# Two of four W2 operands of an expert product start 32 bytes further on, with a table of scan constants moved to another pool

## The chip, the cores and the metric

The kernel runs on one core of a Trainium2 chip. The metric is the time that the device takes for one execution, in microseconds (us), as the median of several runs. The two kernels compute the same thing with the same instructions; only places in the on-chip memory (SBUF, 128 partitions, addresses counted in bytes within a partition) differ.

## What is computed

An attention with a decaying state gives x (3072 tokens of 384 numbers). A first mixture multiplies `(x @ w1) * (x @ w2)` by `w3` and `w_out`. A second one weighs 8 experts by a gate that is balanced eight times over rows and columns, and this is where most of the time goes:

```python
def _moe2_ref(x, w_gate, w1, w2):
    logits = x @ w_gate
    P = np.exp(logits - logits.max())
    for _ in range(8):
        P /= P.sum(1, keepdims=True) + 1e-09
        P /= P.sum(0, keepdims=True) + 1e-09
        P *= N / E
    out = np.zeros((N, D), dtype=np.float32)
    for e in range(E):                       # 8 experts
        h = np.maximum(x @ w1[e], 0.0)       # 384 -> 1024
        out += P[:, e:e + 1] * (h @ w2[e])   # 1024 -> 384
    return out
```

## The kernel before

**Stages.** For about 400 us the attention runs beside the first mixture (`START` and the loop over `s`). Then `N` = 64 phases follow, 8 experts times 2 halves of the inner 1024 times 4 batches of 768 tokens. A phase has two products on TensorE. The *first product* (`phase`, `z_prod`, tiles `zp`) is `x @ w1` in 15 combined block products; its operands are `w1c` (stationary) and `xc` (streamed, 256 columns). After it, ScalarE and VectorE make from each block of `h` a high part `hh` and a low part `hl` (`h_hi`, `h_lo`). The *second product* (`y_fill`, tiles `yp`) is `h @ w2`. It belongs to the phase before and is mixed in between the steps of the first product by a written-out table (`YN`), in `unit`s.

**One unit.** `unit(b_, h_, i, j)` issues three matmuls into the same accumulator: `hh` against the high part of W2 (`w2h`), `hh` against its low part (`w2l`), and `hl` against `w2h`. The 128x128 slice of `hh` or `hl` is stationary; the W2 row block `w_[:, i, :]`, 384 columns of 4 bytes = 1536 bytes a partition, is streamed. `j` runs over 0 and 1 and picks one of a pair of W2 tiles, so the streamed tiles follow each other as h0, l0, h0, h1, l1, h1 and so on (0 and 1 are the pair's first and second tile). A phase has 24 units, 72 matmuls; 64 phases have 4608.

**W2 tiles.** `sp_w2(i)` makes `w2h{k}` and `w2l{k}`, k = i mod 4, each of 2 x 384 numbers (3072 bytes a partition). k = 0 and 1 are one pair and live in the pool `m1`, which is stacked from the upper end of the SBUF; k = 2 and 3 are the other pair, in the pool `m2` at the lower end. Pairs alternate.

**Places.** A pool lays its tiles one behind the other. `spaced` asks for an unused tile ahead of a tag if the table `GAPS` names it, of so many 4-byte numbers a partition, or behind it for a tag with `+`. In the program as built, all streamed operands of both products (`w2h`, `w2l`, `xc`) begin 96 bytes past a multiple of 256, and all stationary ones (`hh`, `hl`, `w1c`) 160 bytes past one. In blocks of 64 bytes, each stream begins 32 bytes into a block and ends 32 bytes into one. In the first mixture the operands (`xhl`, `gh`, `gl` and `w1h`, `w1l`, `w2h`, `w2l`, `w34h`, `w34l`) all begin 96 bytes past a multiple of 256.

**The scans' constants.** `d1` (529 numbers of 2 bytes) is an operand of the two scans of the attention (`scan_f`, `scan_g`). It lies in `const`, the lowest pool, which stays for the whole kernel.

Of the kernel before, what the change touches and what calls it, by code (L numbers as in the profile page):

```python
# [11 lines left out]
F32 = mybir.dt.float32  # L12
F32R = mybir.dt.float32r
BF16 = mybir.dt.bfloat16
# [47 lines left out]
def tile_rwkv_moe_sinkhorn_moe(  # L62
# [18 lines left out]
    nc = tc.nc  # L81
    B, H, S, D = SHAPE
    NT, DM = out.shape
    P = 128
# [21 lines left out]
    def mm(o, lhsT, rhs, start, stop, pos=None, tr=False, skip=False):  # L106
# [5 lines left out]
        if tr:  # L112
# [3 lines left out]
    const = ctx.enter_context(tc.tile_pool(name="const", bufs=1))  # L116
    ident = const.tile([P, P], F32, name="ident")
    mask = const.tile([P, DP], F32, name="mask")
    eye = const.tile([P, DP], F32, name="eye")
    d1 = const.tile([P, 16 * 33 + 1], BF16, name="d1")  # L120
    GP = 32
    gate = const.tile([P, KD, GP], F32, name="gate")
    lowb = const.tile([P, 1], F32, name="lowb")
# [5 lines left out]
    nc.gpsimd.memset(ident, 1.0)  # L129
    nc.gpsimd.affine_select(out=ident, in_=ident, compare_op=ALU.is_equal, fill=0.0,  # L130
                            base=0, pattern=[[-1, P]], channel_multiplier=1)
    nc.vector.memset(d1, 0.0)
    nc.vector.memset(d1[:, 0:528].rearrange("p (b s) -> p b s", s=33)[:, :, 0:1], 1.0)
    nc.vector.memset(d1[:, 528:529], 1.0)
    nc.gpsimd.memset(mask, 1.0)
    for c in range(2):
        nc.scalar.activation(eye[64 * c:64 * c + 64, :], ident[64 * c:64 * c + 64, 64 * c:64 * c + 64], AF.Copy)
# [7 lines left out]
    mw = st_mw.enter_context(tc.tile_pool(name="mw", bufs=1))  # L145
    st_attn = ExitStack()
    att = st_attn.enter_context(tc.tile_pool(name="att", bufs=1))
    st_ps = ExitStack()
    ps = st_ps.enter_context(tc.tile_pool(name="ps", bufs=1, space=PSUM))
    st_pa = ExitStack()  # L150
# [467 lines left out]
        return sums, high, low  # L618

    w1raw, w2raw, w1c, w2c, xc, xd = {}, {}, {}, {}, {}, {}  # L620
    GAPS = {'hh': 32, 'hl+': 32, 'w2h2': 16, 'w2l3+': 16, 'w1c00': 16, 'xc0': 48, 'w1c10': 16, 'xc1': 48, 'w1c01': 16, 'w1c13+': 16}

    def spaced(pool, shape, dtype, tag, name, **kw):
        n_ = GAPS.pop(tag, 0)
        if n_:
            pool.tile([P, n_], F32, name="gap_" + tag)
        t = pool.tile(shape, dtype, tag=tag, name=name, **kw)
        n_ = GAPS.pop(tag + "+", 0)
        if n_:
            pool.tile([P, n_], F32, name="gap_after_" + tag)  # L630
        return t
# [619 lines left out]
```

## Time and profile before

| what | value |
|---|---|
| median of 3 runs | 1918.84 us (1918.38 to 1919.31) |
| the profiled execution | 1919.88 us |
| its span, first to last instruction | 1918.2 us |
| TensorE busy in the span | 1891.9 us, 99% |
| VectorE, ScalarE, GpSimd busy | 72%, 36%, 34% |
| granted TensorE clock | 1.00, the 2.4 GHz level |

TensorE has two rows in a profile: PE, the streaming matmul, and PEld, the load of the stationary operand, which runs beside it. The recorded length of a matmul includes its way through the array and overlaps with the next one, so what one costs is the distance from its start to the next start. The median is 1.04 us below the profiled execution, and the span 1.68 us below it.

### The profile page before, as it was taken

Reading aid. Unit: us, or ns where it says so; the run is one execution under the profiler, and the core shown is the slowest. Engines: PE = TensorE matmul, PEld = TensorE weight load, DVE = VectorE, ACT = ScalarE, POOL = GpSimd, SP = SyncE. Lnnn points to the kernel's source line nnn. Section 1 sums busy time; section 2 is a strip of 40 time slices with the busy share of each in tenths; the row PEclk is TensorE's granted clock in tenths of the full one; section 3 lists DMA queues with packets and bytes.
Section 4 is the critical chain, followed back from the end, with each engine's and each line's share of the span. In section 5 each row is a group of like instructions: output and inputs, shape, how many; then the busy total and the mean of one; then the engine's idle time right before and its main releaser. Section 6 shows DMA issues by size and latency. Waiting matters only on the chain.

```text
span 1918.2 us, 38115 instructions
## 1 busy us (share of the span) xinstructions
PE 1891.9 (99%) x15499; PEld 1843.2 (96%) x15499; DVE 1377.1 (72%) x2409; ACT 685.0 (36%) x1322; POOL 648.2 (34%) x867
## 2 busy tenths in 40 slices
PE   6999999999999999999999999999999999999999
PEld 3799999999999999999999999999999999999999
DVE  7865777766887887766767777767676777767666
ACT  6733333344333333333333333333333333333322
POOL 6766666634431323132222222222323231312200
PEclk9999999999999999999999999999999999999999
DMA  9622444346655555555655555545555555555563
GB/s 369 238 85 92 136 133 139 110 146 223 233 183 200 183 201 192 197 185 179 217 176 205 180 203 183 205 173 197 187 192 192 193 190 196 196 181 185 176 204 120
DMA packets 90494, 353.76 MB, mean 184 GB/s; under 512 B 10384, under 2 KB 34256, under 8 KB 64592
## 3 DMA queue, kind: packets, MB, share of 16 engines
q1 hardware_dynamic: 90320, 351.34, 52.8%
q8 instruction: 122, 2.00, 0.4%
q14 instruction: 52, 0.43, 0.1%
HBM read 329.67 MB, written 20.45 MB: 183 GB/s over the span
## 4 chain that ended last, share of the span: by engine, by line
PE 94%; DVE 2%; DMA 2%; ACT 1%; issue 0%; SPq 0%; DVEq 0%; ACTq 0%
PE yp L114 41%; PE zp L114 34%; PE po L114 5%; PE pa L114 5%; PE pb L114 5%; PE yt L114 1%; DMA raw<-in_moe_w_dram 1%; PE w34ps L114 1%; PE sc L114 1%; PE trn L114 1%; DMA nat_kn<-in_kn_dram 1%; PE up L114 0%; PE pl L114 0%; DVE cvp L229 0%; DVE Sn L384 0%
## 5 line engine op out<-in xcount | busy, mean ns | idle before, releaser
L114 PE MATMUL zp<-xc,w1c 128*128 128x256 f32 x5760 | 793.0, 277 | 0.9 <-DVE ct L906 0.6
L114 PEld LDWEIGHTS zp<-xc,w1c 128*128 128x128 f32 x5760 | 766.5, 188 | 4.4 <-DVE ct L909 1.0
L114 PE MATMUL yp<-w2h,hl 128*128 128x384 f32 x1536 | 515.3, 336 | 0.6 <-DVE hl L903 0.6
L114 PE MATMUL yp<-w2l,hh 128*128 128x384 f32 x1536 | 514.6, 335 | 0.0
L114 PE MATMUL yp<-w2h,hh 128*128 128x384 f32 x1536 | 513.1, 334 | 0.0
L898 ACT ACTIVATE hh<-ct 128x512 fp32r<-128x512 f32 x384 | 236.1, 630 | 526.5 <-DVE ct L906 265.9
L906 DVE TENSOR_TENSOR ct<-ct,zp 128x512 f32<-128x512 f32 x576 | 377.0, 680 | 47.2 <-PE zp L114 42.4
L616 POOL TENSOR_TENSOR w1c<-w1s,w1c 128x512 fp32r<-128x512 f32 (+1 forms) x120 | 127.4, 1062 | 779.6 <-ACT w1c L612 779.6
L913 ACT ACTIVATE ct<-zp 128x512 f32<-128x512 f32 x256 | 153.4, 599 | 440.8 <-PE zp L114 440.8
L114 PEld LDWEIGHTS yp<-w2h,hl 128*128 128x128 f32 x1536 | 288.3, 188 | 1.1 <-DVE hl L903 0.9
L114 PEld LDWEIGHTS yp<-w2h,hh 128*128 128x128 f32 x1536 | 288.4, 188 | 0.2 <-issue 0.2
L114 PEld LDWEIGHTS yp<-w2l,hh 128*128 128x128 f32 x1536 | 288.3, 188 | 0.0
L1078 DVE SCALAR_TENSOR_TENSOR acc<-yp,Pm,acc 128x384 f32<-128x384 f32 x336 | 205.5, 612 | 103.6 <-PE yp L114 103.5
L903 DVE SCALAR_TENSOR_TENSOR hl<-ct,hh 128x512 fp32r<-128x512 f32 x384 | 275.8, 731 | 0.0
L909 DVE TENSOR_TENSOR ct<-ct,zp 128x512 f32<-128x512 f32 x128 | 87.9, 687 | 162.9 <-PE zp L114 162.9
L909 DVE TENSOR_TENSOR ct<-zp,ct 128x512 f32<-128x512 f32 x128 | 88.3, 690 | 74.4 <-ACT ct L913 60.8
L616 POOL TENSOR_TENSOR w1c<-w1raw,w1c 128x128 fp32r<-128x128 f32 (+1 forms) x90 | 56.5, 628 | 195.4 <-ACT w1c L612 195.4
L608 POOL TENSOR_TENSOR w1s<-w1raw 128x128 f32<-128x128 f32 x240 | 120.8, 524 | 0.2
L483 POOL TENSOR_TENSOR gl<-gs,gh 128x384 fp32r<-128x384 f32 x64 | 74.2, 1161 | 109.5 <-ACT gh L479 109.5
L114 PE MATMUL pa<-xhl,w1h 128*128 128x384 f32 x384 | 101.7, 345 | 0.9 <-ACT w34s L255 0.9
L114 PE MATMUL pb<-xhl,w2h 128*128 128x384 f32 x384 | 98.1, 336 | 0.4 <-DVE cv L230 0.4
L474 DVE TENSOR_TENSOR gs<-pb,asb 128x384 f32<-128x384 f32 x64 | 35.4, 553 | 72.0 <-PE pb L114 50.1
(130 smaller groups left out, 1905.3 us busy)
## 6 DMA issues: line engine op xcount, KB each, us to landing
xc<-xd SPq DMA_DIRECT2D x192, 1024.0 KB, 4.9
xc<-xd SPq DMA_DIRECT2D x64, 768.0 KB, 4.2
xd<-x2s SPq DMA_DIRECT2D x53, 256.0 KB, 2.8
w1raw<-in_e_w_dram SPq DMA_DIRECT2D x32, 384.0 KB, 3.2
w2raw<-in_e_w_dram SPq DMA_DIRECT2D x32, 384.0 KB, 3.1
raw<-in_moe_w_dram SPq DMA_DIRECT2D x8, 1024.0 KB, 10.1
nat_w<-in_w_dram SPq DMA_DIRECT2D x24, 264.5 KB, 3.5
nat_k<-in_kt_dram SPq DMA_DIRECT2D x24, 256.0 KB, 4.1
```

The lines of the kernel that those rows point to most:

```text
L114: nc.tensor.matmul(o, lhsT, rhs, start=start, stop=stop, **kw)
L474: nc.vector.tensor_tensor(t, m_t.pop(("pb", blk, f)), m_t.pop(("asb", blk, f)), op=ALU.mult)
L483: nc.gpsimd.tensor_tensor(gl[:, f, :], m_t.pop(("gs", blk, f)), gh[:, f, :].bitcast(F32), op=ALU.subtract)
L608: eng.tensor_tensor(tmp_[:, many.index(r), :], at_(a), at_(b), op=ALU.add if sg == 1 else ALU.subtract)
L616: eng.tensor_tensor(lo[:, d0:d1, :], sv, hi[:, d0:d1, :].bitcast(F32), op=ALU.subtract)
L898: nc.scalar.activation(hh, src, AF.Relu)
L903: nc.vector.scalar_tensor_tensor(hl, src, 0.0, hh.bitcast(F32), op0=ALU.max, op1=ALU.subtract)
L906: nc.vector.tensor_tensor(o, a, b_, op=ALU.add)
L909: nc.vector.tensor_tensor(o, a, b_, op=ALU.subtract)
L913: nc.scalar.activation(t, src, AF.Copy)
L1078: nc.vector.scalar_tensor_tensor(dst, yp, so["Pm"][:, tt, e:e + 1], dst, op0=ALU.mult, op1=ALU.add)
```

## The change

The table gets four more entries, each for one W2 tile: a gap of 8 numbers (32 bytes) ahead of the low part of a pair's first tile, and one of 56 (224 bytes) ahead of the low part of its second, so that 256 bytes are inserted for a pair. The room comes from `d1`, which leaves `const` for the attention's pool `att`; an unused tile of 64 bytes stays at its old place. The three memsets that fill `d1` are written further down.

```diff
-    d1 = const.tile([P, 16 * 33 + 1], BF16, name="d1")
+    const.tile([P, 16], F32, name="gap_const")
@@
-    nc.vector.memset(d1, 0.0)
-    nc.vector.memset(d1[:, 0:528].rearrange("p (b s) -> p b s", s=33)[:, :, 0:1], 1.0)
-    nc.vector.memset(d1[:, 528:529], 1.0)
@@
     att = st_attn.enter_context(tc.tile_pool(name="att", bufs=1))
+    d1 = att.tile([P, 16 * 33 + 1], BF16, name="d1")
+    nc.vector.memset(d1, 0.0)
+    nc.vector.memset(d1[:, 0:528].rearrange("p (b s) -> p b s", s=33)[:, :, 0:1], 1.0)
+    nc.vector.memset(d1[:, 528:529], 1.0)
@@
-    GAPS = {'hh': 32, 'hl+': 32, 'w2h2': 16, 'w2l3+': 16, 'w1c00': 16, ...
+    GAPS = {'hh': 32, 'hl+': 32, 'w2l0': 8, 'w2l1': 56, 'w2h2': 16, 'w2l2': 8, 'w2l3': 56, 'w2l3+': 16, 'w1c00': 16, ...
```

The places in the two programs as built, in bytes past a multiple of 256:

| tile | before | after |
|---|---|---|
| `w2h0`, `w2h2` (high part, first of a pair) | 96 | 96 |
| `w2l0`, `w2l2` (low part, first) | 96 | 128 |
| `w2h1`, `w2h3` (high part, second) | 96 | 128 |
| `w2l1`, `w2l3` (low part, second) | 96 | 96 |
| `xc`, `hh`, `hl`, `w1c` | 96, 160, 160, 160 | the same |
| buffers of the attention | | each 64 bytes further on |
| `d1` | 128 | 96 |

Other tiles move by whole multiples of 256 bytes (256, 768 or 1024 down) or not at all. On every engine the instructions stand in the same order and carry the same waits. On TensorE, at the first two units of the second product (the number behind a tile's name counts tiles in the program; the figure ahead of it, 0 or 1, is the tile of the pair), before:

```order
L114 MATMUL yp_6332<-w2h0_6153,hh_6283 128x384
L114 MATMUL yp_6332<-w2l0_6154,hh_6283 128x384
L114 MATMUL yp_6332<-w2h0_6153,hl_6284 128x384
L114 MATMUL yp_6332<-w2h1_6197,hh_6283 128x384
L114 MATMUL yp_6332<-w2l1_6198,hh_6283 128x384
L114 MATMUL yp_6332<-w2h1_6197,hl_6284 128x384
```

The same place after:

```order
L114 MATMUL yp_6335<-w2h0_6154,hh_6286 128x384
L114 MATMUL yp_6335<-w2l0_6156,hh_6286 128x384
L114 MATMUL yp_6335<-w2h0_6154,hl_6287 128x384
L114 MATMUL yp_6335<-w2h1_6199,hh_6286 128x384
L114 MATMUL yp_6335<-w2l1_6201,hh_6286 128x384
L114 MATMUL yp_6335<-w2h1_6199,hl_6287 128x384
```

Nothing moved; the numbers differ because gaps count as tiles. In these six rows the streamed operands begin 96, 96, 96, 96, 96, 96 bytes past a multiple of 256 before, and 96, 128, 96, 128, 96, 128 after: from matmul to matmul the start alternates between the middle of a 64-byte block and its beginning.

## Rows read from the trace of the kernel before

**Rows 1.** The page's first part: busy time, share of the span, instructions.

```profile
PE 1891.9 (99%) x15499; PEld 1843.2 (96%) x15499; DVE 1377.1 (72%) x2409; ACT 685.0 (36%) x1322; POOL 648.2 (34%) x867
```

**Rows 2.** The page's chain that ended last, by engine.

```profile
PE 94%; DVE 2%; DMA 2%; ACT 1%; issue 0%; SPq 0%; DVEq 0%; ACTq 0%
```

**Rows 3.** Busy time in the stretch of the 64 phases: length, engines, clock, DMA.

```profile
464.20:1914.80 1450.60, 1449.50 (x10331) 1444.95 (x10329) 1045.70 (x1715) 477.45 (x883) 365.95 (x589) 1.00 0.55 191
```

**Rows 4.** TensorE's waits from 464 us on: us in total, times, longest.

```profile
PE yp L114 <- DVE hl L903: 0.6, 1, 0.6
PE zp L114 <- DVE ct L909: 0.3, 1, 0.3
```

**Rows 5.** The page's groups of both products: busy, mean ns, idle before.

```profile
L114 PE MATMUL zp<-xc,w1c 128*128 128x256 f32 x5760 | 793.0, 277 | 0.9 <-DVE ct L906 0.6
...
L114 PE MATMUL yp<-w2h,hl 128*128 128x384 f32 x1536 | 515.3, 336 | 0.6 <-DVE hl L903 0.6
L114 PE MATMUL yp<-w2l,hh 128*128 128x384 f32 x1536 | 514.6, 335 | 0.0
L114 PE MATMUL yp<-w2h,hh 128*128 128x384 f32 x1536 | 513.1, 334 | 0.0
```

**Rows 6.** Timeline of TensorE in mid-stage: start us, length us, matmul, how many.

```profile
1001.20 0.85 PE L114 MATMUL zp<-xc,w1c 128*128 128x256 f32 x6
1001.88 0.33 PE L114 MATMUL yp<-w2h,hh 128*128 128x384 f32 x1
1002.05 0.34 PE L114 MATMUL yp<-w2l,hh 128*128 128x384 f32 x1
1002.23 0.34 PE L114 MATMUL yp<-w2h,hl 128*128 128x384 f32 x1
...
1003.27 0.34 PE L114 MATMUL yp<-w2h,hl 128*128 128x384 f32 x1
1003.44 0.28 PE L114 MATMUL zp<-xc,w1c 128*128 128x256 f32 x1
```

**Rows 7.** The same view, last 78 matmuls of the second product, first and last.

```profile
1901.00 0.33 PE L114 MATMUL yp<-w2h,hh 128*128 128x384 f32 x1
...
1914.35 0.34 PE L114 MATMUL yp<-w2h,hl 128*128 128x384 f32 x1
```

**Rows 8.** Matmuls of `yp` by operand: duration ns min/median/max, first and last start.

```profile
L114 PE MATMUL yp<-w2h,hh x1536: 332/332/443, 464.3 to 1914.0; 128*128 128x384 f32 x192
...
L114 PE MATMUL yp<-w2l,hh x1536: 332/335/339, 464.5 to 1914.2; 128*128 128x384 f32 x192
```

**Rows 9.** Timeline of TensorE in the first mixture's last product.

```profile
403.51 0.33 PE L114 MATMUL po<-gh,w34l 128*128 128x384 f32 x1
...
404.55 0.33 PE L114 MATMUL po<-gh,w34l 128*128 128x384 f32 x1
```

**Rows 10.** VectorE's timeline: one scan from each of `nat_w`'s two buffers.

```profile
120.65 1.25 DVE L279 TENSOR_TENSOR_SCAN Ft<-nat_w,d 128x528 f32<-128x528 f32 x1
```

**Rows 11.** The same view, a later stretch: the other buffer's turn.

```profile
129.25 1.26 DVE L279 TENSOR_TENSOR_SCAN Ft<-nat_w,d 128x528 f32<-128x528 f32 x1 [0.72 <-POOL Rt L312]
```

**Rows 12.** The memsets of `d1` and the scans that read it.

```profile
L283 DVE TENSOR_TENSOR_SCAN Gt<-nat_w,d x24: 1242/1582/2300, 3.6 to 377.6; 128x527 f32<-128x527 f32 x24
L279 DVE TENSOR_TENSOR_SCAN Ft<-nat_w,d x24: 1232/1490/2100, 4.8 to 375.3; 128x528 f32<-128x528 f32 x24
L132 DVE MEMSET d<- x1: 499/499/499, 1.1 to 1.1; 128x529 bf16 x1
```

More of the change, by code (lines that the diff above doesn't have):

```diff
@@ L620, in tile_rwkv_moe_sinkhorn_moe @@
     w1raw, w2raw, w1c, w2c, xc, xd = {}, {}, {}, {}, {}, {}
-    GAPS = {'hh': 32, 'hl+': 32, 'w2h2': 16, 'w2l3+': 16, 'w1c00': 16, 'xc0': 48, 'w1c10': 16, 'xc1': 48, 'w1c01': 16, 'w1c13+': 16}
+    GAPS = {'hh': 32, 'hl+': 32, 'w2l0': 8, 'w2l1': 56, 'w2h2': 16, 'w2l2': 8, 'w2l3': 56, 'w2l3+': 16, 'w1c00': 16, 'xc0': 48, 'w1c10': 16, 'xc1': 48, 'w1c01': 16, 'w1c13+': 16}
     def spaced(pool, shape, dtype, tag, name, **kw):
```

## The prediction, made before the result was known

> **What bounds the kernel now.** Read the busy shares first: TensorE is busy 99% of the span, VectorE 72%, the others far less [rows 1], and the chain of work that ended last lies on TensorE for 94% [rows 2]. That could still hide a stage with another limit, so look at the stage that the change touches. In the 1450.6 us of the 64 phases TensorE is busy for 1449.5 [rows 3], and its list of waits there has two entries, of 0.6 and 0.3 us [rows 4]. Nothing else sets the time of this stage: it is the number of matmuls times the distance from one start to the next. VectorE is idle for 1450.6 - 1045.7 = 404.9 us of it.
>
> The distances come from the timeline. Six matmuls of the first product take 1001.20 to 1001.88, 0.68 / 6 = 113.3 ns each; nine of the second take 1001.88 to 1003.44, 1.56 / 9 = 173.3 ns [rows 6]. The last 78 of the second product, with nothing between them, give 77 distances in 13.35 us, 173.4 ns [rows 7]. The clock granted is 1.00 [rows 3], its 2.4 GHz level, at which 256 columns are 106.7 ns and 384 are 160.0. So a matmul of the first product pays 6.7 ns (16 clocks) beyond its columns and one of the second 13.3 ns (32 clocks). The check: 5760 x 113.3 + 4608 x 173.3 = 652.6 + 798.6 = 1451.2 us with the counts of [rows 5], the length of the stage. 4608 x 13.3 = 61.3 us is all that a better place for W2 could win, if every overhead went.
>
> **What the change adds, removes and moves.** No instruction, no wait and no transfer is added, taken away or reordered on any engine, SP's and GpSimd's queues among them; so no wait can take the place of another except through a changed duration. Three things have a new place.
>
> *The memsets and scans of the constants.* The three memsets follow the same VectorE instruction as before, the big one 499 ns long [rows 12]. The 48 scans read `d1` from a start that is 32 bytes into a 64-byte block instead of at its beginning. Does VectorE care? The two buffers of `nat_w` lie one 32 bytes into a block and the other at the beginning of one, and a scan from each takes 1.26 us [rows 11] and 1.25 us [rows 10] when GpSimd leaves it alone: a difference of 10 ns on 48 scans, 0.5 us of VectorE's time, beside a TensorE that waits elsewhere. I take nothing; were the scans late, the bound is 0.5 us either way.
>
> *The buffers of the attention and the tiles that go down by 256, 768 or 1024 bytes.* These keep their place to the next multiple of 64 or of 256. I take nothing: the second product and the first mixture's last product have their stationary operand at 160 and 96 past a multiple of 256, the streamed one at 96 in both, and both run at the same pace, 6 distances in 1.04 us, 173.3 ns, in the latter [rows 9]. A shift by whole 64-byte blocks between the two operands has no price for a stream of 384 columns.
>
> *The W2 tiles.* This is the whole of the sum. `w2l` of a pair's first tile is streamed in 768 of the 1536 matmuls of hh on w2l, `w2h` of the second in 768 + 768 of the other two groups [rows 5]: 2304 matmuls, half of the product, begin at the start of a 64-byte block instead of 32 bytes into it. No row of the trace shows a streamed operand of this kind in such a place, so the price must be bounded. Below: it may lose all its overhead, 13.3 ns, or 2304 x 13.3 = 30.6 us. Above: nothing excludes a loss, and the nearest size for one is the step in which the overheads come. 6.7 and 13.3 ns are two and four steps of 3.3 ns, which is 8 clocks or 32 bytes of a stream; the recorded lengths of the second product's matmuls also come in two sizes that differ by 3 ns, 332 and 335 [rows 8]. A shift by just 32 bytes should act in such steps.
>
> Which way? Half-used blocks are the argument for a gain. 1024 bytes that begin 32 into a block touch 17 blocks of 64, and 17 x 16 clocks = 272 = 113.3 ns, the first product's distance to the clock. 1536 bytes touch 25 blocks, 166.7 ns, and the row shows 173.3: one block too many, as if the stream were taken in a piece of 256 columns and one of 128 (17 + 9 = 26 blocks). So the fit is good but not complete, and a fixed price of 16 clocks for each piece of up to 256 columns fits the same two numbers with no role for the start. I therefore take the smallest step for the forecast: one step of 3.3 ns on each of the 2304, 7.7 us. Against the profiled execution that is 1919.9 - 7.7 = 1912.2 us; its time stood 1.04 us above the median of the runs, so 1911.2 us for the median. TensorE's gain isn't taken back by another engine: VectorE's 404.9 us of idle time cover it many times.
>
> A page of the Trainium skill speaks against this. SBUF — State Buffer, section Specifications (TRN2), gives SBUF lines of 16 bytes and asks for at least two hits in a line. A start at 96 and one at 128 are both at the beginning of such a line, so by that rule the streams cost what they cost, and the time stays at 1918.8 us. No row here shows whether 16 bytes or 64 is the unit that a stream pays for.
>
> **The rivals.** *The start doesn't matter.* The overhead is a fixed price of each piece or of the handover between matmuls, and a stream costs 173.3 ns wherever it begins: 1918.8 us. For it: that 64 bytes make no difference between [rows 6] and [rows 9], and that the fixed price fits the two distances. Against it: only that the half block does so too.
>
> *All of the overhead goes.* If half blocks are the whole cause, an aligned stream costs 24 x 16 clocks = 160.0 ns, and 30.6 us go: 1888.2 us. For it, 17 x 16; against it, the block too many, and that some fixed price for a matmul would have to be nil.
>
> *Slower: the handover meets the same half block.* Before, a stream's last 32 bytes lie in the first half of a block and the next stream's first in the second half: the halves alternate through the handover. After, they meet in the same half at nearly every handover of the second product: h0 ends in a first half and l0 begins in one, l0 ends in a second half and h0 begins in one. If the two halves are read in turn and a repeat costs one step, it costs 3.3 ns at 2304 handovers if one kind of repeat is bad, +7.7 us or 1926.5 us, and at all 4608 if both are, +15.4 us or 1934.2 us. It decides as soon as more repeats cost a step than shifted streams save one. For it: the step is 32 bytes of stream. Against it: before, the halves alternate already and four steps are paid all the same.
>
> **How the numbers follow.** One or two steps off the shifted streams: 0.37 (two steps would be 1903.5 us); all of the overhead: 0.11; no effect: 0.25; one step more on half of the handovers: 0.18; on all: 0.09. The likeliest gives 1911.2 us. A range of 8 in 10 leaves out the largest gain (0.11) and the largest loss (0.09): from three steps saved, 1895.8, to 1926.5 with the spread of the runs, so 1895 to 1928 us. Both signs hold much of this; the forecast's own range is 1903 to 1912. What a measurement of this kernel can tell from no change is about 0.2%, 3.8 us. Faster by more than that: 0.37 + 0.11 = 0.48; within it 0.25; slower 0.18 + 0.09 = 0.27.
>
> **What would show it.** In the profile of the changed kernel the last 78 matmuls of the second product should take 77 distances of 173.4 - 1.7 = 171.7 ns on average, 13.22 us instead of 13.35; 160-ns distances on every other matmul would speak for the half blocks, 173.3 throughout for the fixed price, and more for the repeat. The first product must keep 113.3 ns, and the first 464 us must not move by more than 0.5 us. I am wrong in the mechanism if a matmul on an unshifted tile changes its distance, and in the bound if the gain stands in TensorE's distances but not in the time.

## The result: slower, and mostly where nothing was moved

The changed kernel takes 1939.03 us, median of four runs (1938.82 to 1939.78), beside 1918.78 us for the kernel before (1918.38 to 1919.31): a ratio of 1.0103, 95% interval 1.0091 to 1.0116. The profiled execution of after is the run of 1939.78 us; its span is 1938.1 us, 19.9 us more than before's 1918.2.

The page of after, first part (busy time, share of the span, instructions), beside [rows 1], and its groups of both products (busy us, mean ns of one, idle before), beside [rows 5]:

```profile
PE 1911.3 (99%) x15499; PEld 1864.0 (96%) x15499; DVE 1381.7 (71%) x2409; ACT 687.2 (35%) x1322; POOL 647.0 (33%) x867
...
L114 PE MATMUL zp<-xc,w1c 128*128 128x256 f32 x5760 | 807.2, 280 | 0.9 <-DVE ct L907 0.6
...
L114 PE MATMUL yp<-w2h,hh 128*128 128x384 f32 x1536 | 518.5, 338 | 0.0
L114 PE MATMUL yp<-w2h,hl 128*128 128x384 f32 x1536 | 517.2, 337 | 0.5 <-DVE hl L904 0.5
L114 PE MATMUL yp<-w2l,hh 128*128 128x384 f32 x1536 | 517.0, 337 | 0.0
```

TensorE is as full as before and busy for 19.4 us longer. The largest group to grow is `zp`, the first product: 793.0 to 807.2 us, though neither its streams nor its stationary tiles moved. The three groups of `yp` gain 9.7 us together (records of neighbouring matmuls overlap, so the groups add up to more than the 19.4). TensorE's waits in the 64 phases are still two (us in total, times, longest), as in [rows 4], so no wait has come in:

```profile
PE yp L114 <- DVE hl L904: 0.5, 1, 0.5
PE zp L114 <- DVE ct L910: 0.3, 1, 0.3
```

Now the timeline of TensorE in after (start us, length us, matmul, how many), where [rows 6] had 113.3 and 173.3 ns:

```profile
600.90 0.87 PE L114 MATMUL zp<-xc,w1c 128*128 128x256 f32 x6
601.61 0.34 PE L114 MATMUL yp<-w2h,hh 128*128 128x384 f32 x1
...
602.66 0.84 PE L114 MATMUL zp<-xc,w1c 128*128 128x256 f32 x6
603.34 0.33 PE L114 MATMUL yp<-w2h,hh 128*128 128x384 f32 x1
...
604.38 0.87 PE L114 MATMUL zp<-xc,w1c 128*128 128x256 f32 x6
605.08 0.34 PE L114 MATMUL yp<-w2h,hh 128*128 128x384 f32 x1
```

Six matmuls of the first product take 0.71, 0.68 and 0.70 us: 118, 113 and 117 ns each. Below, a *stretch* is a run of matmuls of one product with none of the other between them, and a *rhythm* the distance that such a run keeps. It is one kernel, one set of places, and two rhythms; a stretch that begins in one mostly stays in it. The last 78 matmuls of the second product, which answer [rows 7]:

```profile
1920.90 0.34 PE L114 MATMUL yp<-w2h,hh 128*128 128x384 f32 x1
...
1934.25 0.34 PE L114 MATMUL yp<-w2h,hl 128*128 128x384 f32 x1
```

That is 77 distances in 13.35 us, 173.4 ns (173.3 from the exact starts), as before, although half of these streams have moved. On average the second product, left alone, runs as it did. Single distances don't: they go from 171 to 176 ns, where before shows 173 and 174 behind the first one.

Where the 19.9 us lie, from the start times of all matmuls sorted by neighbours (all distances of each kind added up, after minus before): matmuls of `zp` +13.9 us; the first matmul of `yp` behind a stretch of `zp`, 170 ns before and some 175 after, +4.1; the other matmuls of `yp` +2.4. From these 20.4 goes half a microsecond by which the first `zp` starts earlier (441.3 instead of 441.8 us).

The kernel before, and e1 too, gave two values at the same granted clock, about 1919 and about 1929 us; the higher has no profile and no known cause, and while e5 to e8 were taken it was the only one (1928.74 us), so for those four the spans and distances count here and not the ratio (e8's would be 0.9978).

### The profile page after: what moved, and what is told of

It is laid out like the page before. It is cut to its first block, busy times and chain, and to the rows that moved or that the text cites. A ratio compares the mean times of both kernels' runs of the same rounds, so it can differ in the third digit from the quotient of the medians.

```text
span 1938.1 us, 38115 instructions
## 1 busy us (share of the span) xinstructions
PE 1911.3 (99%) x15499; PEld 1864.0 (96%) x15499; DVE 1381.7 (71%) x2409; ACT 687.2 (35%) x1322; POOL 647.0 (33%) x867
## 4 chain that ended last, share of the span: by engine, by line
PE 95%; DVE 2%; DMA 1%; ACT 1%; issue 0%; SPq 0%; DVEq 0%; ACTq 0%
PE yp L114 41%; PE zp L114 35%; PE po L114 5%; PE pa L114 5%; PE pb L114 5%; PE w34ps L114 1%; PE yt L114 1%; PE sc L114 1%; PE trn L114 1%; DMA nat_kn<-in_kn_dram 1%; PE up L114 1%; DMA raw<-in_moe_w_dram 0%; PE pl L114 0%; DVE Sn L385 0%; DVE cvp L230 0%
## 5 line engine op out<-in xcount | busy, mean ns | idle before, releaser
L114 PE MATMUL zp<-xc,w1c 128*128 128x256 f32 x5760 | 807.2, 280 | 0.9 <-DVE ct L907 0.6
L114 PEld LDWEIGHTS zp<-xc,w1c 128*128 128x128 f32 x5760 | 776.7, 188 | 3.5 <-DVE ct L910 0.9
L114 PE MATMUL yp<-w2h,hh 128*128 128x384 f32 x1536 | 518.5, 338 | 0.0
```

Source lines behind the costliest of these rows:

```text
L114: nc.tensor.matmul(o, lhsT, rhs, start=start, stop=stop, **kw)
```

## The experiments

A place is told in bytes past a multiple of 256, and the difference is the stationary tile's place minus the stream's. Which tile is loaded while a stream runs can be read from the trace: the load for a matmul starts together with the matmul ahead of it. In run e6 (below), the timeline of the weight loads, and of the matmuls:

```profile
601.43 0.83 PEld L114 LDWEIGHTS zp<-xc,w1c 128*128 128x128 f32 x6
602.20 0.19 PEld L114 LDWEIGHTS yp<-w2h,hh 128*128 128x128 f32 x1
```

```profile
601.43 0.34 PE L114 MATMUL yp<-w2h,hl 128*128 128x384 f32 x1
601.61 0.87 PE L114 MATMUL zp<-xc,w1c 128*128 128x256 f32 x6
602.31 0.34 PE L114 MATMUL yp<-w2h,hh 128*128 128x384 f32 x1
```

The load for the first `zp` begins at 601.43, with the last `yp`, and that for the first `yp` at 602.20, with the last `zp`. So there are four differences: within the first product (w1c and xc), from the first to the second (hh is loaded beside xc), within the second (hh or hl and W2), from the second to the first (w1c is loaded beside W2). Before, all four are 160 - 96 = 64. Runs e1 to e16 have `d1` where after has it and differ from after in the line of gaps alone (a gap of n is 4n bytes), so they all do the same work in the same order. In the table, two differences stand where some W2 tiles have the one and some the other. "zp" and "first yp" are mean distances from start to start in ns: the first leaves out the one distance of 0.8 to 0.9 us that each run has, the second is that of the first `yp` behind a stretch of `zp`, with two values where it depends on the pair's tile (first/second). "last 78" is the mean of the 77 distances at the end.

| kernel | 1st | 1st to 2nd | 2nd | 2nd to 1st | zp | first yp | last 78 | span us |
|---|---|---|---|---|---|---|---|---|
| before | 64 | 64 | 64 | 64 | 114.2 | 170.0 | 173.3 | 1918.2 |
| after | 64 | 64 | 64/32 | 64/32 | 116.6 | 175 | 173.3 | 1938.1 |
| e1 | 64 | 64 | 64 | 64 | 114.2 | 170 | 173.3 | 1917.0 |
| e2 | 64 | 64 | 64/0 | 64/0 | 115.8 | 170/175 | 174.9 | 1931.7 |
| e3 | 64 | 64 | 32 | 32 | 117.7 | 180 | 173.4 | 1945.3 |
| e4 | 64 | 64 | 64/32 | 64 | 116.6 | 175/172 | 175.6 | 1941.5 |
| e5 | 32 | 32 | 32 | 32 | 118.1 | 173/177 | 173.5 | 1948.7 |
| e6 | 64 | 96 | 64 | 32 | 117.9 | 176 | 176.7 | 1952.0 |
| e7 | 64 | 96 | 96 | 64 | 115.7 | 182 | 173.4 | 1936.6 |
| e8, e16 | 64 | 64 | 0 | 0 | 113.8, 114.1 | 175 | 173.4 | 1921.9, 1924.8 |
| e9 | 64 | 64 | 64 | 64 | 114.3 | 170 | 173.3 | 1917.8 |
| e10 | 64 | 32 | 64 | 96 | 117.9 | 176/177 | 176.8 | 1951.7 |
| e11 | 64 | 64 | 64/32 | 64/32 | 116.5 | 174 | 175.4 | 1936.2 |
| e12 | 64 | 64 | 64/32 | 64 | 114.9 | 170 | 175.0 | 1927.6 |
| e13 | 0 | 0 | 0 | 0 | 118.6 | 175/176 | 173.4 | 1949.4 |
| e14 | 128 | 128 | 128 | 128 | 118.7 | 173/178 | 176.0 | 1956.9 |
| e15 | 0 | 0 | 64 | 64 | 118.7 | 182 | 176.8 | 1967.5 |

The granted clock is 1.000 in every one of them, its 2.4 GHz level.

The theories at the start were four: the constants cost; the half of a 64-byte block in which a stream begins (the prediction's idea); the step from one stream's place to the next one's; and the difference between a stream and the stationary tile of its product.

### e1 to e4: which part, and which step

e1 keeps the W2 tiles in their old places and moves only the constants:

```diff
-    GAPS = {..., 'w2l0': 8, 'w2l1': 56, 'w2h2': 16, 'w2l2': 8, 'w2l3': 56, 'w2l3+': 16, ...
+    GAPS = {..., 'w2h2': 16, 'w2l3+': 16, ...
```

> Only the constants of the scans move; no gaps at W2, so every streamed operand begins 96 bytes past a multiple of 256 as in the kernel before. Theory A (a 32-byte step between the starts of streams that follow each other puts TensorE into a slower rhythm, which the first product then keeps): the time of the kernel before, 1918.8 us, first product at 113.3 ns a matmul. Theory C (the constants, or the tiles that went down by 256 to 1024 bytes, are the cause): about 1939 us, first product at about 116.7 ns.

Median 1923.47 us, ratio 0.9996 (0.9961 to 1.0032); the group of `zp` reads as before, and no mean distance in the table has moved (the group of `zp` in e1 stands below). The constants and the tiles that moved by multiples of 64 or 256 along with them are nothing; the gaps at W2 are all of it.

```profile
L114 PE MATMUL zp<-xc,w1c 128*128 128x256 f32 x5760 | 792.9, 277 | 0.9 <-DVE ct L907 0.6 <-DVE ct L910 0.3
```

e2 moves the same tiles by 64 bytes instead of 32, e3 all W2 tiles by 32, e4 all low parts by 32:

```diff
 e2
-    'w2l0': 8, 'w2l1': 56, 'w2h2': 16, 'w2l2': 8, 'w2l3': 56, 'w2l3+': 16
+    'w2l0': 16, 'w2l1': 48, 'w2h2': 16, 'w2l2': 16, 'w2l3': 48, 'w2l3+': 16
 e3
+    'w2h0': 8, 'w2l1+': 56, 'w2h2': 24, 'w2l3+': 8
 e4
+    'w2l0': 8, 'w2h1': 56, 'w2l1': 8, 'w2l1+': 56, 'w2h2': 16, 'w2l2': 8, 'w2h3': 56, 'w2l3': 8, 'w2l3+': 8
```

> The same four W2 tiles begin 64 bytes further on instead of 32 (gaps of 64 and 192 bytes). The start alternates from stream to stream, but always lies in the middle of a 64-byte block. Theory A (32-byte step): 1918.8 us, both paces as before. Theory B (any difference between the starts of streams that follow each other): 1939 us, as with 32.

> All four W2 tiles of both pairs begin 32 bytes further on, at 128 past a multiple of 256; the first product's streams stay at 96. The start changes only where the products hand over to each other. Theory A, with the last handover deciding: each stretch of the first product follows a shifted stream, so all 5760 matmuls run at 117.7 ns instead of 113.3, +25 us, 1944 us. Theory A, with the number of changes deciding: a third of the changes are left (1640 of about 5400), so a third of 20 us, 1926 us. Theory D (the place of the second product's own stream against its stationary operand decides): the second product's own pace changes, the first product stays at 113.3 ns.

> Only the low parts of W2 (w2l0 to w2l3) begin 32 bytes further on; the high parts, which are streamed first and last in each unit, stay. Theory A, with the last handover deciding: each stretch of the first product follows an unshifted stream, so 113.3 ns and 1918.8 us. Theory A, with any change setting the slower rhythm and nothing ending it: as slow as the changed kernel, about 1939 us or, if all matmuls of the first product are caught, 1944 us.

They take 1932.88, 1946.04 and 1942.91 us: ratios of 1.0045, 1.0113 and 1.0097; by span they are 13.5, 27.1 and 23.3 us longer than before. The group of `zp` (busy us, mean ns of one, idle before) in e2:

```profile
L114 PE MATMUL zp<-xc,w1c 128*128 128x256 f32 x5760 | 802.2, 279 | 0.9 <-DVE ct L907 0.6 <-DVE ct L910 0.3
```

In e3:

```profile
L114 PE MATMUL zp<-xc,w1c 128*128 128x256 f32 x5760 | 814.4, 281 | 1.1 <-DVE ct L907 0.6 <-DVE ct L910 0.5
```

In e4:

```profile
L114 PE MATMUL zp<-xc,w1c 128*128 128x256 f32 x5760 | 807.4, 280 | 1.1 <-DVE ct L907 0.6 <-DVE ct L910 0.5
```

e3 is the telling one. All W2 streams begin alike, there is no step between neighbours in the second product, its last stretch keeps 173.4 ns, and yet the first product is slower than in any of the others so far. Take as a stretch's pace the mean of its distances without the first and the last, call it slow at 116.5 ns or more and fast under 115, and look at the 820 stretches of `zp` that stand behind one of `yp`: 812 are slow in e3, and 800 fast in before. Steps between neighbouring streams of the second product are not needed for the loss.

e4 says that the last handover is not all of it either. Each of its stretches of `zp` follows an unshifted stream, for which the theory of the last handover wanted 1918.8 us, and it takes 1942.91 with `zp` at 116.6 ns.

### e5 to e8: streams, stationary tiles, a whole product

e5 moves all streams (W2 and xc) by 32; e6 the second product whole, W2 and hh, hl by 32; e7 only hh and hl by 32; e8 only W2, by 64:

```diff
 e5
+    'hh': 32, 'hl+': 32, 'xc2': 8, 'w2l1+': 56, 'w2h2': 24, 'w2l3+': 8, 'w1c00': 16, 'xc0': 56, 'w1c10': 8, 'xc1': 56, 'w1c01': 8
 e6
+    'hh': 40, 'hl+': 24, 'w2h0': 8, 'w2l1+': 56, 'w2h2': 24, 'w2l3+': 8
 e7
+    'hh': 40, 'hl+': 24, 'w2h2': 16, 'w2l3+': 16
 e8
+    'hh': 32, 'hl+': 32, 'w2h0': 16, 'w2l1+': 48, 'w2h2': 32
```

> Every streamed operand of both products (W2 and xc) begins 32 bytes further on, at 128 past a multiple of 256, the beginning of a 64-byte block; the stationary ones stay at 160. Theory A (a step between the starts of streams that follow each other): no step is left, 1918.8 us, 113.3 and 173.3 ns. Theory H (half-used blocks of 64 bytes, the forecast's argument): less than before, down to 106.7 and 160.0 ns, about 1820 us. Theory S (the start of a stream against its own stationary operand): neither, the paces of both products change, upwards after what the 32-byte step did so far.

> W2 and the second product's stationary operands hh and hl all begin 32 bytes further on, so that within each product streamed and stationary operand stand to each other as before; only between the products there is a step of 32 bytes. Theory A (step between streams): like all of W2 shifted, 1946 us, first product at 117.6 ns. Theory S (streamed against stationary operand of the same matmul): 1918.8 us.

> Only hh and hl begin 32 bytes further on; all streams stay at 96. Theory A (step between streams): 1918.8 us. Theory S (streamed against stationary operand; a changed difference puts TensorE into the slower rhythm): slow, about 1940 us.

> All of W2 begins 64 bytes further on, at 160, where the stationary operands begin; xc stays at 96. The alternating step of 64 cost 13.5 us and the first product found back to 113.3 ns within a few matmuls of each stretch. Theory A: a step only at the handover between the products, again with recovery, between 1919 and 1932 us. If the size of the step doesn't matter: 1946 us as with 32.

Measured: 1950.16, 1954.29, 1937.91 and 1924.22 us. The group of `zp` in e5:

```profile
L114 PE MATMUL zp<-xc,w1c 128*128 128x256 f32 x5760 | 815.5, 281 | 1.0 <-DVE ct L907 0.6 <-DVE ct L910 0.5
```

In e6:

```profile
L114 PE MATMUL zp<-xc,w1c 128*128 128x256 f32 x5760 | 813.3, 281 | 0.8 <-DVE ct L907 0.6 <-DVE ct L910 0.3
```

In e7:

```profile
L114 PE MATMUL zp<-xc,w1c 128*128 128x256 f32 x5760 | 803.3, 279 | 0.9 <-DVE ct L907 0.6 <-DVE ct L910 0.3
```

In e8:

```profile
L114 PE MATMUL zp<-xc,w1c 128*128 128x256 f32 x5760 | 790.8, 276 | 0.8 <-DVE ct L907 0.6 <-DVE ct L910 0.2
```

In e5 every stream begins at the start of a 64-byte block and no step is left between any two of them; it is slow, so neither the half block nor the step of the streams decides alone. In e6 the differences within both products are those of before, and it is slower still, so the difference within a product is not enough either. What e6 changes is the two handovers. In e7 the stretches of `zp` begin slow (117.1 ns on average at the first matmul) and many find back (113.7 at the last but one); in e8 the first product is as fast as before and only the second loses.

### e9 and e10: the other half of the square

e9 moves every operand of both products by 32, so that all differences stay; e10 moves only the first product, the mirror of e6:

```diff
 e9
+    'hh': 40, 'hl+': 24, 'xc2': 8, 'w2l1+': 56, 'w2h2': 24, 'w2l3+': 16, 'w1c00': 24, 'xc0': 48, 'w1c10': 16, 'xc1': 48, 'w1c01': 16, 'w1c13+': 8
 e10
+    'hh': 32, 'hl+': 32, 'xc2': 8, 'w2h0': 56, 'w2h2': 16, 'w2l3+': 24, 'w1c00': 24, 'xc0': 48, 'w1c10': 16, 'xc1': 48, 'w1c01': 16, 'w1c13+': 8
```

> Every streamed tile and every stationary tile of both products begins 32 bytes further on (streamed at 128, stationary at 192 in 256), so that each difference between a stream and a stationary tile, within a product and at each handover, is that of the kernel before. If only these differences count: the first product keeps 113.9 ns, the last stretch of the second 173.3 ns, the first matmul of the second product after the first 170 ns, and the time is that of the kernel before within 2 us. If the place itself counts: the first product goes to 116 to 118 ns and the time is 15 to 35 us above the kernel before.

> Only the first product's operands move: its streams (xc) to 128, its stationary tiles (w1c) to 192; the second product is as before. Within each product all differences stay, at the handovers both change: while the last matmul of a stretch of the second product streams, the load is now 96 bytes on from the stream instead of 64, and at the end of a stretch of the first it is 32 instead of 64. If the handover sets the rhythm of the stretch behind it, as the runs before suggest: first product 116 to 118 ns, second unchanged in its last stretch (173.3), time 12 to 35 us above the kernel before. If only differences within a product count: the time of the kernel before within 2 us.

e9: 1919.49 us, ratio 1.0001 (0.9991 to 1.0010). e10: 1953.77 us, ratio 1.0181 (1.0166 to 1.0196). The group of `zp` in e9:

```profile
L114 PE MATMUL zp<-xc,w1c 128*128 128x256 f32 x5760 | 793.3, 277 | 1.2 <-DVE ct L907 0.6 <-DVE ct L910 0.5
```

The first and the last of its last 78 matmuls, in the timeline of TensorE:

```profile
1900.69 0.33 PE L114 MATMUL yp<-w2h,hh 128*128 128x384 f32 x1
...
1914.03 0.34 PE L114 MATMUL yp<-w2h,hl 128*128 128x384 f32 x1
```

The same two views of e10:

```profile
L114 PE MATMUL zp<-xc,w1c 128*128 128x256 f32 x5760 | 814.8, 281 | 0.9 <-DVE ct L907 0.6 <-DVE ct L910 0.2
```

```profile
1934.30 0.34 PE L114 MATMUL yp<-w2h,hh 128*128 128x384 f32 x1
...
1947.91 0.34 PE L114 MATMUL yp<-w2h,hl 128*128 128x384 f32 x1
```

Before, e9, e6 and e10 make a square: each product at its old places or 32 bytes on. Moved together or not at all: 1917.8 and 1918.2 us of span. Only one moved: 1952.0 and 1951.7. e10's second product has the places of before's, tile for tile, and takes 13.61 / 77 = 176.8 ns where before took 173.3 and where I had expected no change; its first product has the places of e9's and runs at 117.9 instead of 114.3. So in this square a common place counts for nothing, and a product's pace is not settled by its own operands: what lies at the handover between the products is carried on into the stretch behind it, even over 78 matmuls.

### e11 and e12: the change in halves

e11 keeps the shift of the high part of the second tile only, e12 that of the low part of the first only:

```diff
 e11
-    'w2l0': 8, 'w2l1': 56, 'w2h2': 16, 'w2l2': 8, 'w2l3': 56, 'w2l3+': 16
+    'w2h1': 8, 'w2l1': 56, 'w2h2': 16, 'w2h3': 8, 'w2l3': 56, 'w2l3+': 16
 e12
+    'w2l0': 8, 'w2h1': 56, 'w2h2': 16, 'w2l2': 8, 'w2h3': 56, 'w2l3+': 16
```

> Half of the change: only the high part of a pair's second W2 tile is 32 bytes on, the low parts are as before. A matmul of a high part is the one ahead of a stretch of the first product. If the handover sets the rhythm: stretches of the first product behind a shifted high part run at 117.6 ns, those behind an unshifted one at 113.3, mean 115 to 116, and the time keeps half or more of the change's 20 us (+8 to +20). If each change of place between two streams costs by itself, it is about half the change, +10 us, spread over the second product, and the first product keeps 113.9.

> The other half of the change: only the low part of a pair's first W2 tile is 32 bytes on, the high parts are as before. No matmul of a low part stands ahead of a stretch of the first product. If the handover sets the rhythm: the first product keeps 113.9 ns and the time is that of the kernel before within 4 us. If each change of place between two streams costs by itself: about +10 us, as in the run with the high part alone.

e11: 1937.83 us, ratio 1.0097 (1.0082 to 1.0112). e12: 1929.75 us, ratio 1.0055 (1.0040 to 1.0070). The group of `zp` in e11:

```profile
L114 PE MATMUL zp<-xc,w1c 128*128 128x256 f32 x5760 | 806.7, 280 | 1.1 <-DVE ct L907 0.6 <-DVE ct L910 0.5
```

In e12:

```profile
L114 PE MATMUL zp<-xc,w1c 128*128 128x256 f32 x5760 | 797.2, 278 | 0.9 <-DVE ct L907 0.6 <-DVE ct L910 0.3
```

The last matmul ahead of a stretch of `zp` streams a high part. I sorted the stretches by it. In e11, 317 of 318 behind a shifted high part are slow; behind an unshifted one 304 of 502 are fast. In after, 316 of 318 behind a shifted high part are slow, and 187 of 502 behind an unshifted one fast. In e12, where no high part is shifted, 683 of 820 stretches are fast, and the end of a stretch is back at 113.4 ns on average, as in before. That is the handover at work, and e11 alone has nearly all of the change's loss in `zp` (806.7 us beside 807.2).

But the handover is not the whole of what runs ahead. Behind an unshifted high part 314 of 502 stretches are slow in after, too. In e12 every handover from the second product is 64. Where the unit ahead of a stretch of `zp` is one on the pair's second tile and stands alone, 188 of 190 stretches are fast; where a unit on the first tile, with its shifted low part, runs ahead of that one, 124 of 128 are slow. The same last unit and the same handover thus lead to either rhythm, by what ran more than three matmuls earlier.

The rest of my expectation missed. e12 loses 10.4 us where up to 4 were allowed (its four runs lie at 1929 to 1931 us, which the kernel before beside it reached once in 14), 6.4 of them in `yp` by the profile: steps between neighbouring streams of the second product do cost, 1.7 ns on average for each of its matmuls that follows another, while e3, with all W2 tiles shifted alike, loses nothing there. And the halves don't add: 18.5 and 10.4 us, the whole 20.2.

### e13 to e16: which differences hold the fast rhythm

e13 has all streams 64 on, so that all differences are 0; e14 64 back, all 128; e15 moves only xc by 64; e16 is e8 again:

```diff
 e13
+    'xc2': 16, 'w2l1+': 48, 'w2h2': 32, 'w1c00': 16, 'xc0': 64, 'xc1': 64
 e14
+    'xc2': 48, 'w2l1+': 16, 'w2l3+': 32, 'w1c00': 16, 'xc0': 32, 'w1c10': 32, 'xc1': 32, 'w1c01': 32
 e15
+    'xc2': 16, 'w2h0': 48, 'w2h2': 16, 'w2l3+': 16, 'w1c00': 16, 'xc0': 64, 'xc1': 64
```

> All streams 64 bytes on, at 160, where all stationary tiles lie: every difference between a stream and the load beside it, within the products and at the handovers, is 0 instead of 64. If a change of the difference between neighbouring matmuls is what puts the first product into its slow rhythm, one difference everywhere keeps it out: first product 113.3 to 113.9 ns, last stretch of the second 173.3, time that of the kernel before within 3 us. If the size of the difference counts (32 bad, 64 good): 0 stands beside 32 and the first product may go to 116 to 118, time +10 to +30 us.

> All streams 64 bytes back, at 32: every difference is 128 instead of 64. If one difference everywhere is enough: first product 113.3 to 113.9 ns, time that of the kernel before within 3 us. If the size of the difference counts and 64 is a good one by itself: 116 to 118 and +10 to +30 us. Together with the run at 0 and the earlier one at 32 (where all differences were equal too and the time was 1.1% above before) it tells whether differences that are multiples of 64 bytes are alike.

> Only the first product's streams are 64 bytes on, at 160: its differences are 0 and, at its end, 0; the second product keeps 64, also at its end. If steps of 64 bytes between neighbours keep the rhythm: first product 113.3 to 114 ns, time that of the kernel before within 5 us. If any change of the difference between the products disturbs it: first product 116 ns and more, +10 us and more.

> The second product's streams alone at 160, as in an earlier run, beside the three others on one chip. If it is as fast as the kernel before or faster: within 3 us of it, or below. Since its span there was 5 us longer than that of the kernel before (first matmul behind a stretch of the first product 175 ns instead of 170), +4 to +6 us is expected here, and that it is no better version.

Measured: 1949.99 us, ratio 1.0147 (1.0115 to 1.0179); 1957.89, 1.0188 (1.0157 to 1.0220); 1969.32, 1.0248 (1.0216 to 1.0280), the slowest of all; 1925.95, 1.0020 (0.9988 to 1.0051). The group of `zp` in e13:

```profile
L114 PE MATMUL zp<-xc,w1c 128*128 128x256 f32 x5760 | 819.0, 281 | 1.0 <-DVE ct L907 0.5 <-DVE ct L910 0.5
```

In e14:

```profile
L114 PE MATMUL zp<-xc,w1c 128*128 128x256 f32 x5760 | 819.6, 281 | 1.0 <-DVE ct L907 0.6 <-DVE ct L910 0.4
```

In e15:

```profile
L114 PE MATMUL zp<-xc,w1c 128*128 128x256 f32 x5760 | 819.0, 282 | 0.9 <-DVE ct L907 0.5 <-DVE ct L910 0.4
```

In e16:

```profile
L114 PE MATMUL zp<-xc,w1c 128*128 128x256 f32 x5760 | 792.4, 277 | 0.8 <-DVE ct L907 0.6 <-DVE ct L910 0.3
```

One difference everywhere is not enough: at 0 and 128, as at 32 in e5, the first product is slow. Within the first product 64 is the only one of 0, 32, 64 and 128 with which it was fast, and with 64 there it goes with the handover from the second product wherever all W2 tiles lie alike: 64 keeps it fast or lets many stretches come back (before, e7, e9), 0 kept it fast (e8, e16), 32 or 96 does not (e3, e6, e10). The second product's last stretch, with 64 within it, goes with the handover from the first in the same way: 173.3 ns behind 64 (before, e1, e9), 176.7 to 176.8 behind 96, 32 or 0 (e6, e10, e15). Where the W2 tiles differ among themselves (after, e2, e4, e11, e12), the steps within the stretch ahead count as well, as e4 and e12 show. A step of 64 is no safe one either, as e15 shows. e16, beside its own kernel before, is no better version, and a little slower than the 4 to 6 us that were expected: by the profiles it saves 2.6 us on the first `zp` behind a stretch of `yp` (116.8 to 113.7 ns) and loses 2 on the other matmuls of `zp` and 8 in `yp`. Nothing tried beats the kernel before.

What stays open: why. Which access waits for which, why 64 is the good difference, why in e2 only 58 of 318 stretches behind a handover of 0 are fast (and 429 of 502 behind one of 64), and why the second product's last stretch, at differences of 0, 32 and 96 within it, takes 173.4 to 173.5 ns whatever came ahead, but with 128 takes 176.0. A stream and a load that start together and collide at certain distances in SBUF would fit the square of e6, e9 and e10; no run shows the collision itself. The load records hint at it: beside matmuls of `zp` in the slow rhythm, 722 of 2708 loads in after are 192 ns long, and none in the fast one, where they are 187 or 188.

## Why the prediction was wrong, point by point

**What bounds the kernel.** Right: TensorE's matmuls times their distances, and no new wait. That the sum of counts and paces came within 0.6 us of the stage was in part luck: 78 of its 5760 matmuls of `zp` run ahead of 464.2 us, and the matmuls at a handover don't keep the two paces. The first `yp` behind a stretch of `zp` takes 170 ns in before (1001.88 to 1002.05 in [rows 6]), the first `zp` behind one of `yp` 116.8. So the trace of before already showed that what runs ahead changes a matmul's distance, and the prediction read past it.

**The constants and the tiles moved by multiples of 64 and 256.** Right that they cost nothing here: e1's span is 1917.0 us beside 1918.2. But the general sentence behind it, that a shift by whole 64-byte blocks between two operands has no price for a stream of 384 columns, was wrong. It was read from two uniform products, [rows 7, 9], at differences of 64 and 0. At 0 it holds in a uniform stretch (e13's last 78: 173.4 ns), at 128 it does not (e14's: 176.0), and in the mixture of the two products it fails: e13 is 1.5% slower, e14 1.9%, e15 2.5%.

**"This is the whole of the sum": the step that failed.** The working counted the 2304 matmuls whose stream moves and let every other keep its distance. The 5760 matmuls of the first product carry two thirds of the loss, 13.9 us, and 4.1 us more lie on first matmuls of `yp`, which stream w2h0 or w2h1 alike. The prediction had named this as the sign that its mechanism is wrong: a matmul on an unshifted tile that changes its distance. The last 78 matmuls gave no gain either: 173.3 ns on average, the value it had put down for a fixed price, though not the 173.3 throughout that this asks for, since single distances go from 171 to 176. What the runs show in place of that term: the loss comes from where the W2 streams lie against the tiles loaded beside them (e1 without the gaps at W2 loses nothing), the shift of the second tile's high part alone brings nearly all of the loss in `zp` (e11), and it falls on whole stretches behind the moved streams.

**The size of a step, 3.3 ns.** The sizes that appear are of that order: 113.3 to 118.0 ns within the stretches of `zp` in after, 173.3 to 176.7 in a slow run of `yp`. But they fall on whole stretches, in both products, and not on each shifted stream.

**The rival "the start doesn't matter".** True of the place by itself: e9 moves every start by 32 bytes and takes 1919.49 us. False of the place beside the other operand. The Trainium skill's page SBUF — State Buffer, section Specifications (TRN2), with its 16-byte lines, would leave all these kernels alike; e9 agrees with it, e6 and e10, which differ from e9 by 32 bytes in one product, are 1.8% off.

**The rival "all of the overhead goes".** e5 has every stream at the start of a block, and its distances are 118.1 and 173.5 ns, not 106.7 and 160.0.

**The rival "slower: the handover".** Its sign was right, and the word too, but it was another handover. It priced the handovers between neighbouring matmuls of `yp` by the half block in which they meet, 7.7 or 15.4 us; after's last 78 matmuls, 77 such handovers, show no price on average (e11's and e12's, with half the change each, do: 175.4 and 175.0 ns), and e5, in which no two halves meet at a handover and which is slow all the same, speaks against the half block. The handover that costs most is that between the products, and what it costs lies in the stretch behind it.

**The range.** Its upper end, 1928, came from one step on half of the handovers of the second product, with a loss on all of them, 1934, left out as the last tenth. Both stop at the second product. A bound from the rows would have been that any matmul of the stage may take one step more: 10368 x 3.3 = 34 us, 1953 us, and of the kernels tried only e14, e15 and, by a microsecond, e6 and e10 lie beyond it.

## What to carry to other kernels

When two products alternate on TensorE and each load runs beside the stream ahead, price a change of place by all pairs that run side by side, those across the handover included, and for every matmul of the stage, not just the moved ones. Look for the signs in the trace of before: there the first matmul behind a handover already kept another distance. Move all operands together if something must move (32 bytes on all of them: no change), and look at start-to-start distances per neighbour, since neither the busy share (99% throughout) nor the waits show this loss. A pace read from a long uniform run says little about the same matmuls in a mixture.

## What the hardware showed that was not expected

- A stretch of matmuls has more than one steady rhythm with the same operands at the same places: 113.3 or 118.0 ns on average at 256 columns (after), 173.3 or 176.8 ns at 384 (before and e10), all at a granted clock of 1.000. What ran ahead goes with it, further back than the last matmul (e12), and a stretch of 78 does not leave it (e6, e10).
- The place of the operands relative to each other, modulo 256 bytes, is worth up to 2.5% of this kernel (e15) in a stage that is bound by TensorE; a common shift of 32 bytes nothing (e9).
- The load of the next stationary tile starts 2 to 5 ns after the start of the stream ahead in 99% of the pairs, in both rhythms (before and after).
